# A ring of 27 banks of exponentials in place of a scaled copy of V, with a second side bank and no credit rule in the last sets

## The chip, the cores and the metric

The kernel runs on one core of one Trainium2 chip. The metric is the device time of one execution in microseconds (us). Runs of a kernel are summed up by their median.

## The reference

One transformer block with adaptive layer norm: S = 2048 tokens, D = 512, H = 32 heads of 16, F = 1792, all in bf16.

```python
mod = (silu(c) @ w_mod) -> sa, ca, ga, sb, cb, gb        # six rows of 512
h = layernorm(x) * (1 + ca) + sa
q, k, v = split(h @ wqkv)                                 # 32 heads, Dh = 16
p = softmax(q @ k.T * Dh ** -0.5)                         # 2048 x 2048 for each head
x = x + ga * (concat(p @ v) @ wo)
h = layernorm(x) * (1 + cb) + sb
x = x + gb * ((gelu(h @ w_gate) * (h @ w_up)) @ w_down)
```

## The kernel before

**Tiles and sets.** The 2048 queries are cut into seven sets: two of 512 tokens, three of 256, two of 128 (`SETS`). A unit is one set and one group of four heads (`qd`, eight of them); the two last sets share their first five units, which are 256 wide. A unit walks over the keys in rounds. A round is four banks, one per head, of 128x512 scores. In all there are 2048 banks, in a fixed order; `pos` is the number of banks issued so far, and `ends[k]` the position at which set k is done. `ends[4]` is 1792: the last two sets are the last 256 banks.

**From scores to PV.** TensorE writes scores (QK) to `scp`, six PSUM banks used as two groups of three in turn. ScalarE takes a group's banks in one exponential and writes them to `E`, a ring of `NSL` = 12 banks in SBUF. TensorE then multiplies them with V (`vaug`, which has a column of ones for the denominator) and accumulates in `pv`, one PSUM bank. QK of a group is issued only when the ring has free places for it, that is, when the rounds that held these places have been through PV.

**Vector rounds.** Some rounds are made on VectorE instead. Of a group of three banks ScalarE then takes two, and VectorE the third. One TENSOR_SCALAR turns scores into the bits of a bf16 number y whose exponent is right and whose mantissa is linear (`BITS_C`). When four banks are there (128x2048), three more steps follow (`power_task`): `mant` keeps y's mantissa bits and sets the exponent of one (a mask and an OR), `square` multiplies that with y, and `expo` keeps only y's exponent (a mask). The power of two is the sum of both, the square times 0.496 and the exponent part times one. So such a round goes through PV twice: the exponent part with `vaug`, the square with `vs`, a copy of V scaled by `SQUARE_W`. The copies are made by `scale_v`, 16 instructions, each after its part of V. A vector round is opened only when VectorE's queue is short, buffers are free, no earlier one is overdue, V's scaled copy is there, and, from `LATE_AT` = `ends[4]` on, when the credit of the side work is under `CREDIT` = 1024. Only a full group of three can give a bank to VectorE.

**Side work.** Everything else (projections of later heads, output projection, layer norm, FFN of finished sets) is a list of generators. Each yields matmuls into one PSUM bank, `mi`, and then empties it with VectorE instructions. Side work earns credit with every bank of scores, by what is left of it and when it is due, and spends it in TensorE columns; a high credit means that it is behind. TensorE is kept awake with filler matmuls on the identity when its recent work falls under a bound (`FILL`).

**Order.** The program is one list per engine, put in order by a scheduler in the kernel file, which keeps modelled times of all engines (`free`, `probe`). At each step it issues QK as soon as its banks and places are free, else PV, side work or filler. The scheduler runs when the kernel is built; the chip runs the finished lists, with semaphores.

**End.** The last sets' leftovers are run by `tail`: output projection and FFN of the last set, mixed with the rest of the FFN of the set before it.

All matmuls are recorded by line 318, all ScalarE instructions by line 336, and on VectorE two-tensor operations by line 340, tensor-scalar ones by 348, copies by 357. So groups of one line are told apart by tile names.

Of the kernel before, what the change touches and what calls it, by code (L numbers as in the profile page):

```python
# [6 lines left out]
ALU = mybir.AluOpType  # L7
# [9 lines left out]
H = 32  # L17
# [17 lines left out]
QS = 5  # L35
CH = 3
SC = 2 * CH
NSL = 12
assert NSL % CH == 0
LEAD = 5  # L40
CREDIT = 1024
LATE_AT = lambda ends: ends[4]
AHEAD = 24
NEAR = 8
FIRST = 0
# [12 lines left out]
EXP_SCALE = float(np.log(2.0) / OCT)  # L58
Q_SCALE = float(0.25 * np.log2(np.e) * OCT)

SQUARE_W = 0.49609375
BITS_C = float(128 * (127 - 0.58035))
MANT, ONE, EXPO = 0x7F, 0x3F80, 0xFF80

COMPUTE = ("pe", "act", "dve", "pool")
ALLENG = ("sp",) + COMPUTE
# [362 lines left out]
class _Kernel(_Recorder):  # L429
# [12 lines left out]
    def alloc(self):  # L442
# [32 lines left out]
        self.bufs += [(mreg[:, 4096 + 2048 * i:6144 + 2048 * i], "modB") for i in range(4)]  # L475
        self.bufs.append((wreg[:, 4096:6144], ("q", 3, 3)))
        self.held = set()
        self.flowing = self.closing = False
        self.vs = sb("vs", [P, NKT, H * VW], BF16)
        self.wo = sb("wo", [P, 8, D], BF16)  # L480
        self.E = sb("E", [P, NSL, 512], BF16)
        self.onorm = sb("onorm", [P, 8, 512], BF16)
# [232 lines left out]
    def side_v(self, g, dc):  # L715
        mi = self.mi[:, :]

        def part(t):
            for dci in range(NDC):
                self.mm(mi[:, P * t:P * t + P], self.hT[:, dci, 512 * g + P * t:512 * g + P * t + P],  # L720
                        self.wqkv[:, dci, 1024 + P * dc:1024 + P * dc + P],
                        start=(dci == 0), stop=(dci == NDC - 1))
        for t in range(4):
            yield 512, lambda t=t: part(t)
        dst = self.vaug[:, 4 * g:4 * g + 4, VW * 8 * dc:VW * 8 * dc + VW * 8]
        self.copy("dve", dst.rearrange("p t (h c) -> p t h c", c=VW)[:, :, :, 0:DH],
                  mi.rearrange("p (t h c) -> p t h c", t=4, c=DH))
        self.done(("v", g, dc))
        if not self.dry:
            self.task([lambda: self.scale_v(g, dc)], ("vs", g, dc))  # L730
        yield END

    def scale_v(self, g, dc):
        t, c = slice(4 * g, 4 * g + 4), slice(VW * 8 * dc, VW * 8 * dc + VW * 8)
        self.ts("dve", self.vs[:, t, c], self.vaug[:, t, c], SQUARE_W, None, ALU.mult)

    def side_t(self, src, n, h, out, mod):
        pt = self.mi[:, :].bitcast(BF16)
        w = P * n

        def part(i):
            for t in range(n):
                self.transpose(pt[:, w * i + P * t:w * i + P * t + P],
                               src(t)[:, P * (2 * h + i):P * (2 * h + i) + P], self.ident[:, :])
        for i in range(2):
            yield w, lambda i=i: part(i)
        for i in range(2):
            dc = 2 * h + i
            self.modulate("dve", out(dc), pt[:, w * i:w * i + w], mod, dc)
        yield END  # L750

    def after(self, keys):
        return lambda: all(k in self.have for k in keys)
# [135 lines left out]
    def side_wo(self, gi):  # L889
        q0, W = SETS[gi]  # L890
        n = W // P
        tiles = [q0 // P + i for i in range(n)]
        mi = self.mi[:, :]
        yield from self.until("wo")
        for i in range(n):
            for qd in range(8):
                yield from self.until(("onorm", gi, qd))
                yield 512, lambda i=i, qd=qd: self.wo_mm(mi, gi, i, qd)
            self.wo_fin(mi, tiles[i])
            if not self.dry:  # L900
                self.task([lambda t=tiles[i]: self.ln_stat(t)], ("st2", tiles[i]))
            yield END
        if not self.dry:
            self.done(("wo", gi))
            self.task(self.ln2_steps(gi), ("ln2", gi), self.after([("st2", t) for t in tiles]))

    def side_ffn(self, gi, part=None):
# [1 line left out]
        q0, W = SETS[gi]  # L909
        n = W // P  # L910
        tiles = [q0 // P + i for i in range(n)]
        mi = self.mi[:, :]
        c0 = BCOL[gi]
        prod = self.prodT if W == 512 else self.prodL
        flow = gi < FLOW
# [32 lines left out]
            yield from self.side_t(lambda t: self.normed(gi, t), n, h,  # L948
                                   lambda dc: self.t2T[:, dc, c0:c0 + W], self.modB)

        def up(x, ci, sub, after=()):
            for s, fc in enumerate(sub):
                for dci in range(NDC):
                    if flow:
                        lhs = ring[(nch * x + ci) % 4][:, dci, P * (fc % 2):P * (fc % 2) + P]
                    else:
                        lhs = self.up_w((self.wg, self.wu)[x], fc, dci)
                    yield W, lambda s=s, lhs=lhs, dci=dci, aft=after if s == dci == 0 else (): self.mm(
                        mi[:, W * s:W * s + W], lhs, self.t2T[:, dci, c0:c0 + W], start=(dci == 0), stop=(dci == NDC - 1),
                        after=aft)  # L960
# [11 lines left out]
        if part is not None:  # L972
            for ci in range(part):
                fcs = chunks[ci]
                m = len(fcs)
                g, w = self.gw[:, ci % 2, 0, 0:m * W], self.gw[:, ci % 2, 1, 0:m * W]
                yield from up(0, ci, fcs)
                self.copy("dve", g, mi[:, 0:W * m])
                if not self.dry:
                    self.task([lambda g=g, w=w: self.tt("dve", w, g, g, ALU.mult),  # L980
                               lambda w=w: self.ts("dve", w, w, GELU_C, 1.0, ALU.mult, ALU.add),
                               lambda g=g, w=w: self.tt("dve", w, w, g, ALU.mult),
                               ("act", lambda w=w: self.act(w, w, ACT.Tanh, scale=TANH_C0))], ("gelu", gi, ci))
                yield END
            for ci in range(part):
                fcs = chunks[ci]
                m = len(fcs)
                g, w = self.gw[:, ci % 2, 0, 0:m * W], self.gw[:, ci % 2, 1, 0:m * W]
                yield from self.until(("gelu", gi, ci))
                yield from up(1, ci, fcs)  # L990
                self.stt(w, w, 1.0, mi[:, 0:W * m], ALU.add, ALU.mult)
                self.stt(place(fcs), split(w, m), 0.5, split(g, m), ALU.mult, ALU.mult)
                yield END
            self.done(("part", gi))
            return
        for i in range(3):
            load_down(i)
        for ci in range(len(chunks)):
            for sub in banks(ci):
                yield from up(0, ci, sub)  # L1000
                self.copy("dve", place(sub), split(mi[:, 0:W * len(sub)], len(sub)))
                yield END
            load(ci + 4)
# [3 lines left out]
        yield from self.until(("gelu", gi))  # L1007
        for ci in range(len(chunks)):
            for sub in banks(ci):
                yield from up(1, ci, sub, (place(sub),))  # L1010
                self.tt("dve", place(sub), split(mi[:, 0:W * len(sub)], len(sub)), place(sub), ALU.mult)
                yield END
            load(nch + ci + 4)
        for i in range(n):
            for fc in range(NFC):
                yield 512, lambda i=i, fc=fc: self.mm(
                    mi, prod[:, fc, P * i:P * i + P], (self.wdst if flow else self.wd)[fc // 2][:, fc % 2, :], start=(fc == 0), stop=(fc == NFC - 1))
            self.down_fin(mi, tiles[i])
            yield END
# [124 lines left out]
    def stream(self):  # L1144
        self.split = True
        self.tasks = []
        self.task([lambda: self.scale_v(0, 0)], ("vs", 0, 0))
        self.live = {}
        self.have = {("k", 0, 0), ("q", 0, 0), ("v", 0, 0)}
        self.credit = 0  # L1150
# [132 lines left out]
        while cg <= group[units[-1]]:  # L1283
# [8 lines left out]
            self.background(t)  # L1292

            tq = None
            mem, after = take(CH - 1 if pos < nsplit + 12 and c % 2 else CH)
            s0 = CH * (c % 2)
            if mem:
                e0 = 0 if e + len(mem) > NSL else e
                if all(owner.get(e0 + i, -1) < rp for i in range(len(mem))):
                    tq = self.probe(lambda: self.mm(self.scp[:, s0:s0 + CH, 0:P], *filler))  # L1300
            if tq is not None and tq <= t + 30:
                slack = self.free["act"] - 600 - t
                w = self.next_side()
# [7 lines left out]
                if len(mem) == CH and ("k", 3, 0) in self.have and self.free["dve"] < max(t + 400, self.free["act"]) + 500:  # L1311
# [4 lines left out]
                        if not overdue - {quad["rnd"][0]}:  # L1316
                            g = pick(quad)
                    elif (not overdue and cand and len(self.spare()) > 1 and (pos < LATE_AT(ends) or self.credit < CREDIT) and rounds[cand[0]][2] < pos + 96 and self.backlog() < BACK
                          and ("vs", rounds[cand[0]][1] * (512 // rounds[cand[0]][0][3]) // 4, rounds[cand[0]][0][1] // 2) in self.have
                          and all(k in self.have for k in self.keys(seq[rounds[cand[0]][2]]))):  # L1320
                        rnd = rounds[cand.pop(0)]
                        quad = {"rnd": rnd, "j": [0, 1, 2, 3], "k": self.spare()[0], "ready": [], "n": 2, "slot": None}
# [83 lines left out]
    def pv_mms(self, rnd, acc, src, i, first, last):  # L1406
# [2 lines left out]
        dc, ee = qd // 2, qd % 2  # L1409
        for kk in range(kpb):  # L1410
            kt = r * kpb + kk
            v = (self.vs if i else self.vaug)[:, kt, :]
            for j in range(4):
                h = 8 * dc + 2 * j + ee
                self.mm(acc[32 * j:32 * j + VW, 0:W], v[:, VW * h:VW * h + VW], src[j][:, W * kk:W * kk + W],
# [7 lines left out]
    def power_task(self, q):  # L1423
# [5 lines left out]
            return self.bufs[self.spare()[0] if q["slot"] is None else q["slot"]][0]  # L1429

        def mant():
            self.ts("dve", slot().bitcast(U16), y.bitcast(U16), MANT, ONE, ALU.bitwise_and, ALU.bitwise_or)
            if self.probing is None:
                q["slot"] = self.spare()[0]
                self.held.add(q["slot"])
# [4 lines left out]
                q["ready"].append((1, quarters(slot())))  # L1440

        def expo():
            self.ts("dve", y.bitcast(U16), y.bitcast(U16), EXPO, None, ALU.bitwise_and)
            if self.probing is None:
                q["ready"].append((0, quarters(y)))
        self.task([mant, square, expo], ("shift", q["rnd"][0]),
# [55 lines left out]
    def tail(self, ka, kb):  # L1502

        self.require([("part", ka)])
        self.split = False
        self.act(self.tcol[:, 0:1], self.tcol[:, 0:1], ACT.Gelu_apprx_tanh)
        gens = [self.tail_end(kb), self.tail_ffn(ka, self.pv[:, :], range(0, 4), 0)]
# [140 lines left out]
```

## Time and profile before

| what | us |
|---|---|
| median of 3 runs (lowest, highest) | 856.21 (853.2, 856.58) |
| the profiled execution's own time | 852.99 |
| its span, first to last instruction | 851.2 |
| ScalarE busy | 810.5 (95%) |
| TensorE busy | 747.1 (88%) |
| VectorE busy | 724.0 (85%) |
| mean granted TensorE clock | 0.997 |

The time of an execution is its span and 1.8 us around it. Busy shares are means over the whole span; the stages differ, which the views by stretches of time show. Groups of instructions give the count, the busy time, the mean of one, and the idle time of their engine just ahead of them with what ended it.

### The profile page before, as it was taken

The numbers are of one execution on the slowest core, as the hardware profiler recorded it, in microseconds if no ns is written. First come the engines' busy times: TensorE is split into PE (matmuls) and PEld (weight loads), VectorE is DVE, ScalarE is ACT, GpSimd is POOL, SyncE is SP. The second block draws the span as 40 slices with busy tenths as digits, with TensorE's granted clock in tenths as the row PEclk, the third lists the DMA queues.
The fourth block names the chain that finished last, engine by engine and source line by source line (L and its number), as shares of the span: only waits on it lengthen the run. The fifth ranks groups of instructions, "written<-read, shape, count | busy, mean of one in ns | idle before, by whom it ended". The sixth has DMA issues, their size and how long they took to land.

```text
span 851.2 us, 29704 instructions
## 1 busy us (share of the span) xinstructions
PE 747.1 (88%) x13466; PEld 292.1 (34%) x13471; DVE 724.0 (85%) x1307; ACT 810.5 (95%) x738; POOL 4.5 (1%) x12
## 2 busy tenths in 40 slices
PE   7888989888888978899998989998898889888887
PEld 3333232322222222222333323433443443344455
DVE  7857999999999987999999999999898989735764
ACT  5999999999999999999999999999998999999982
POOL 1000000000000000000000000000000000000000
PEclk9999999999999999999999999999999999999999
DMA  8100000000012111110003212103451431500000
GB/s 284 39 25 13 9 9 9 10 9 8 9 45 66 55 35 33 46 33 21 23 9 94 71 45 55 48 23 105 122 155 47 144 97 55 144 10 6 22 6 13
DMA packets 76360, 43.71 MB, mean 51 GB/s; under 512 B 20557, under 2 KB 74634, under 8 KB 76234
## 3 DMA queue, kind: packets, MB, share of 16 engines
q1 hardware_dynamic: 76232, 41.82, 17.4%
q8 instruction: 105, 1.72, 0.8%
q14 instruction: 21, 0.17, 0.1%
q10 hardware_dynamic: 2, 0.00, 0.0%
HBM read 39.18 MB, written 2.61 MB: 49 GB/s over the span
## 4 chain that ended last, share of the span: by engine, by line
ACT 69%; PE 14%; DVE 9%; DMA 4%; SPq 1%; issue 1%; DVEq 0%
ACT E L336 66%; PE ps_mi L318 6%; PE ps_sc L318 6%; PE ps_pv L318 2%; ACT hreg L336 2%; DVE mreg L348 2%; DMA rb<-scr_rec 1%; DMA scr_rec<-rden 1%; ACT L336 1%; SPq L386 1%; DMA den<-scr_den 1%; DMA scr_den<-osb 1%; DVE mreg L340 1%; DVE dreg L348 1%; DVE hreg L357 1%
## 5 line engine op out<-in xcount | busy, mean ns | idle before, releaser
L336 ACT ACTIVATE E<-ps_sc 128x1024 bf16<-128x1024 f32 (+2 forms) x698 | 765.1, 1294 | 19.2 <-PE ps_sc L318 18.5
L318 PE MATMUL ps_sc<-qT,kmo 32*128 32x256 bf16 (+2 forms) x1664 | 194.3, 299 | 21.9 <-ACT E L336 19.5
L318 PE MATMUL ps_sc<-qT,kme 32*128 32x256 bf16 (+2 forms) x1600 | 188.4, 304 | 26.8 <-ACT E L336 23.8
L348 DVE TENSOR_SCALAR mreg<-ps_sc 128x512 uint16<-128x512 f32 x232 | 157.1, 686 | 23.6 <-PE ps_sc L318 21.4
L318 PE MATMUL ps_pv<-E,vaug 128*17 128x256 bf16 (+2 forms) x2620 | 165.9, 300 | 8.3 <-DVE osb L357 4.3
L318 PE MATMUL ps_mi<-wreg,mreg 128*32 128x256 bf16 (+2 forms) x2048 | 112.0, 319 | 17.6 <-DVE hreg L340 8.5
L348 DVE TENSOR_SCALAR dreg<-ps_sc 128x512 uint16<-128x512 f32 x140 | 94.8, 686 | 14.7 <-PE ps_sc L318 13.0
L318 PEld LDWEIGHTS ps_sc<-qT,kme 32*128 32x128 bf16 x1600 | 51.8, 92 | 140.0 <-ACT E L336 116.2
L318 PEld LDWEIGHTS ps_sc<-qT,kmo 32*128 32x128 bf16 x1664 | 54.5, 92 | 123.8 <-ACT E L336 90.6
L318 PEld LDWEIGHTS ps_pv<-E,vaug 128*17 128x17 bf16 x2620 | 55.1, 89 | 86.6 <-issue 47.2
L318 PEld LDWEIGHTS ps_mi<-wreg,mreg 128*32 128x32 bf16 x2048 | 44.1, 95 | 57.4 <-issue 17.5
L348 DVE TENSOR_SCALAR mreg<-mreg 128x2048 uint16<-128x2048 uint16 x86 | 58.3, 681 | 0.1
L340 DVE TENSOR_TENSOR hreg<-ps_mi,hreg 128x512 bf16<-128x512 f32 x49 | 33.6, 685 | 13.8 <-PE ps_mi L318 13.7
L357 DVE CAST hreg<-ps_mi 128x512 bf16<-128x512 f32 x49 | 33.6, 685 | 10.3 <-PE ps_mi L318 10.1
L318 PE MATMUL ps_mi<-hreg,wreg 128*32 128x512 bf16 x480 | 38.4, 383 | 1.2 <-DVE vaug L357 0.5
L318 PE MATMUL ps_mi<-wo,onorm 128*32 128x512 bf16 x480 | 37.0, 383 | 1.8 <-DVE xs L340 1.4
L340 DVE TENSOR_TENSOR dreg<-mreg,dreg 128x2048 bf16<-128x2048 bf16 x30 | 36.4, 1215 | 0.0
L318 PE MATMUL ps_mi<-xs,ident 128*32 128x512 bf16 x412 | 32.6, 382 | 1.9 <-DVE hreg L357 1.1
L340 DVE TENSOR_TENSOR mreg<-mreg 128x2048 bf16<-128x2048 bf16 x28 | 33.9, 1212 | 0.1
L340 DVE TENSOR_TENSOR mreg<-dreg,mreg 128x2048 bf16<-128x2048 bf16 x27 | 32.8, 1215 | 0.1
L318 PE MATMUL ps_mi<-mreg,hreg 128*32 128x512 bf16 x384 | 32.4, 384 | 0.0
L340 DVE TENSOR_TENSOR onorm<-osb,rb 128x256 bf16<-128x256 f32 (+2 forms) x51 | 24.6, 485 | 8.7 <-DMA rb<-scr_rec 8.5
(159 smaller groups left out, 684.7 us busy)
## 6 DMA issues: line engine op xcount, KB each, us to landing
mreg<-in_B_w_up_dram SPq DMA_DIRECT2D x32, 256.0 KB, 3.0
mreg<-in_B_w_gate_dram SPq DMA_DIRECT2D x28, 256.0 KB, 3.3
mreg<-in_B_w_down_dram SPq DMA_DIRECT2D x16, 256.0 KB, 2.8
dreg<-in_B_w_down_dram SPq DMA_DIRECT2D x12, 256.0 KB, 5.3
mreg<-in_w_mod_dram SPq DMA_DIRECT2D x1, 2048.0 KB, 12.0
rb<-scr_rec SPq DMA_DIRECT2D x64, 32.0 KB, 1.8
out_dram<-xs SPq DMA_DIRECT2D x16, 128.0 KB, 1.8
rb<-scr_rec SPq DMA_DIRECT2D x116, 16.0 KB, 1.7
```

Of the source, the lines that this page charges most:

```text
L318: return self.rec("pe", lambda e: e.matmul(out, lhsT, rhs, start=start, stop=stop, tile_position=tp), [lhsT, rhs, *after], [out], cost=(n, ...
L336: return self.rec("act", lambda e: e.activation(out, in_, func, scale=scale, **kw), rd, wr, cost=self.cost("act", out, [in_], "act") + load)
L340: return self.rec(eng, lambda e: e.tensor_tensor(out, a, b, op), [a, b], [out], cost=self.cost(eng, out, [a, b], "tt"))
L348: return self.rec(eng, lambda e: e.tensor_scalar(out, a, s1, s2, **kw), rd, [out], cost=self.cost(eng, out, [a], "ts") + (60 if len(rd) > ...
L357: return self.rec(eng, lambda e: e.tensor_copy(out, in_), [in_], [out], cost=self.cost(eng, out, [in_], "ts"))
L386: return e.dma_start(out, in_)
```

## The change

- `vs` and `scale_v` go. The factor is put into the masks: `mant` now sets the exponent of one half (`HALF`), so that the square is halved, and `expo` sets the lowest mantissa bit (`UNIT`), which multiplies the exponent part by 1 + 1/128. The ratio of both is as before, and the common factor is taken out in `BITS_C`. Both PV passes use `vaug`, and a vector round waits for its part of `vaug` instead of `vs`.
- The memory of `vs` (17,408 bytes of each partition) becomes ring: `NSL` is 27, 15 banks of 1024 bytes more.
- `CREDIT` is 5000. The credit is held to 4096 at most, so the rule is never in force.
- From `TWO_AT` = `ends[4]` until the tail, side work uses `mi` and the last bank of `scp` in turn (`bank()`), and every second group has two banks instead of three, as in the first stage, where that bank is the accumulator of a second unit.

```diff
-NSL = 12
+NSL = 27
-CREDIT = 1024
+CREDIT = 5000
 LATE_AT = lambda ends: ends[4]
+TWO_AT = lambda ends: ends[4]
...
-SQUARE_W = 0.49609375
-BITS_C = float(128 * (127 - 0.58035))
-MANT, ONE, EXPO = 0x7F, 0x3F80, 0xFF80
+BITS_C = float(128 * (127 - 0.58035 - np.log2(1 + 2.0 ** -7)))
+MANT, HALF, EXPO, UNIT = 0x7F, 0x3F00, 0xFF80, 0x0001
...
-        self.vs = sb("vs", [P, NKT, H * VW], BF16)
+        self.two = self.flip = False
...
-        if not self.dry:
-            self.task([lambda: self.scale_v(g, dc)], ("vs", g, dc))
...
-    def scale_v(self, g, dc):
-        t, c = slice(4 * g, 4 * g + 4), slice(VW * 8 * dc, VW * 8 * dc + VW * 8)
-        self.ts("dve", self.vs[:, t, c], self.vaug[:, t, c], SQUARE_W, None, ALU.mult)
...
+    def bank(self):
+        if self.dry or not self.two:
+            return self.mi[:, :]
+        self.flip = not self.flip
+        return self.scp[:, SC - 1, :] if self.flip else self.mi[:, :]
...
-        mi = self.mi[:, :]
         yield from self.until("wo")
         for i in range(n):
+            mi = self.bank()
...
-                yield from up(0, ci, fcs)
+                mi = self.bank()
+                yield from up(mi, 0, ci, fcs)
...
-            mem, after = take(CH - 1 if pos < nsplit + 12 and c % 2 else CH)
+            self.two = pos >= TWO_AT(ends)
+            mem, after = take(CH - 1 if (pos < nsplit + 12 or self.two) and c % 2 else CH)
...
-                    tq = self.probe(lambda: self.mm(self.scp[:, s0:s0 + CH, 0:P], *filler))
+                    tq = self.probe(lambda: self.mm(self.scp[:, s0:s0 + len(mem), 0:P], *filler))
...
-                          and ("vs", rounds[cand[0]][1] * (512 // rounds[cand[0]][0][3]) // 4, rounds[cand[0]][0][1] // 2) in self.have
+                          and ("v", rounds[cand[0]][1] * (512 // rounds[cand[0]][0][3]) // 4, rounds[cand[0]][0][1] // 2) in self.have
...
-            v = (self.vs if i else self.vaug)[:, kt, :]
+            v = self.vaug[:, kt, :]
...
-            self.ts("dve", slot().bitcast(U16), y.bitcast(U16), MANT, ONE, ALU.bitwise_and, ALU.bitwise_or)
+            self.ts("dve", slot().bitcast(U16), y.bitcast(U16), MANT, HALF, ALU.bitwise_and, ALU.bitwise_or)
...
-            self.ts("dve", y.bitcast(U16), y.bitcast(U16), EXPO, None, ALU.bitwise_and)
+            self.ts("dve", y.bitcast(U16), y.bitcast(U16), EXPO, UNIT, ALU.bitwise_and, ALU.bitwise_or)
...
 def tail(self, ka, kb):
         self.require([("part", ka)])
+        self.two = False
```

More of the change, by code (lines that the diff above doesn't have):

```diff
@@ L728, in side_v @@
         self.done(("v", g, dc))
-        if not self.dry:
-            self.task([lambda: self.scale_v(g, dc)], ("vs", g, dc))
         yield END
-    def scale_v(self, g, dc):
-        t, c = slice(4 * g, 4 * g + 4), slice(VW * 8 * dc, VW * 8 * dc + VW * 8)
-        self.ts("dve", self.vs[:, t, c], self.vaug[:, t, c], SQUARE_W, None, ALU.mult)
     def side_t(self, src, n, h, out, mod):
-        pt = self.mi[:, :].bitcast(BF16)
+        pt = self.bank().bitcast(BF16)
         w = P * n
@@ L911, in side_ffn @@
         tiles = [q0 // P + i for i in range(n)]
-        mi = self.mi[:, :]
         c0 = BCOL[gi]
@@ L949, in side_ffn, with up @@
                                    lambda dc: self.t2T[:, dc, c0:c0 + W], self.modB)
-        def up(x, ci, sub, after=()):
+        def up(mi, x, ci, sub, after=()):
             for s, fc in enumerate(sub):
@@ L989, in side_ffn @@
                 yield from self.until(("gelu", gi, ci))
-                yield from up(1, ci, fcs)
+                mi = self.bank()
+                yield from up(mi, 1, ci, fcs)
                 self.stt(w, w, 1.0, mi[:, 0:W * m], ALU.add, ALU.mult)
@@ L999, in side_ffn @@
             for sub in banks(ci):
-                yield from up(0, ci, sub)
+                mi = self.bank()
+                yield from up(mi, 0, ci, sub)
                 self.copy("dve", place(sub), split(mi[:, 0:W * len(sub)], len(sub)))
@@ L1009, in side_ffn @@
             for sub in banks(ci):
-                yield from up(1, ci, sub, (place(sub),))
+                mi = self.bank()
+                yield from up(mi, 1, ci, sub, (place(sub),))
                 self.tt("dve", place(sub), split(mi[:, 0:W * len(sub)], len(sub)), place(sub), ALU.mult)
@@ L1014, in side_ffn @@
         for i in range(n):
+            mi = self.bank()
             for fc in range(NFC):
@@ L1146, in stream @@
         self.tasks = []
-        self.task([lambda: self.scale_v(0, 0)], ("vs", 0, 0))
         self.live = {}
```

## The prediction

> **What bounds the kernel now.** I read the page first, for the engine that is never free.
>
> ```profile
> span 851.2 us, 29704 instructions
> PE 747.1 (88%) x13466; PEld 292.1 (34%) x13471; DVE 724.0 (85%) x1307; ACT 810.5 (95%) x738; POOL 4.5 (1%) x12
> L336 ACT ACTIVATE E<-ps_sc 128x1024 bf16<-128x1024 f32 (+2 forms) x698 | 765.1, 1294 | 19.2 <-PE ps_sc L318 18.5
> ```
>
> ScalarE is busy for 810.5 of 851.2 us, and 765.1 of that are exponentials. Little else is left in its row. A change gains by making ScalarE do fewer banks, by filling its few holes, or by shortening what stands behind its last exponential.
>
> Second, the groups by shape, which price one bank (128x512 scores) on either engine:
>
> ```profile
> L336 ACT ACTIVATE E<-ps_sc 128x1536 bf16<-128x1536 f32 x292 | 416.8, 1551 | 4.0 <-PE ps_sc L318 3.8
> L336 ACT ACTIVATE E<-ps_sc 128x1024 bf16<-128x1024 f32 x400 | 392.4, 1119 | 7.9 <-PE ps_sc L318 7.6
> L348 DVE TENSOR_SCALAR mreg<-ps_sc 128x512 uint16<-128x512 f32 x232 | 157.1, 686 | 23.6 <-PE ps_sc L318 21.4
> L348 DVE TENSOR_SCALAR mreg<-mreg 128x2048 uint16<-128x2048 uint16 x86 | 58.3, 681 | 0.1
> L340 DVE TENSOR_TENSOR dreg<-mreg,dreg 128x2048 bf16<-128x2048 bf16 x30 | 36.4, 1215 | 0.0
> L348 DVE TENSOR_SCALAR vs<-vaug 128x544 bf16<-128x544 bf16 x16 | 4.4, 282 | 0.1
> ```
>
> Three banks against two differ by 1551 - 1119 = 432 ns, which is the price of a bank on ScalarE. The instructions overlap, so the fixed part comes from the sum: 292 x 3 + 400 x 2 = 1676 banks x 0.432 = 724 us of the 765.1, and 41 us over 698 instructions is 0.059 us each. A vector round (four banks) costs VectorE 4 x 0.686 + 2 x 0.681 + 1.215 = 5.32 us and relieves ScalarE of 4 x 0.432 = 1.73 us.
>
> Third, busy time in stretches of 20 us, for the place where VectorE is not full (columns PE, PEld, DVE, ACT), and the same for the score banks alone, where the DVE count is the vector banks:
>
> ```profile
> 700.00:720.00 20.00, 18.96 (x405) 8.13 (x400) 18.05 (x29) 18.52 (x18) 0.00 (x0) 1.00 0.23 66
> 740.00:760.00 20.00, 18.06 (x432) 9.12 (x428) 10.30 (x29) 20.00 (x16) 0.00 (x0) 1.00 0.05 10
> 760.00:780.00 20.00, 15.79 (x396) 8.49 (x390) 10.93 (x18) 19.95 (x17) 0.00 (x0) 1.00 0.03 7
> 780.00:800.00 20.00, 18.61 (x520) 9.53 (x520) 12.08 (x23) 19.79 (x19) 0.00 (x0) 1.00 0.08 21
> 800.00:820.00 20.00, 17.53 (x580) 10.05 (x580) 11.88 (x33) 20.00 (x16) 0.00 (x0) 1.00 0.05 9
> ...
> 700.00:720.00 20.00, 6.92 (x108) 2.08 (x108) 7.77 (x12) 18.52 (x18) 1.00 0.23 66
> 740.00:760.00 20.00, 7.17 (x112) 2.08 (x112) 0.00 (x0) 20.00 (x16) 1.00 0.05 10
> 760.00:780.00 20.00, 5.13 (x88) 1.84 (x82) 2.74 (x4) 14.11 (x13) 1.00 0.03 7
> 780.00:800.00 20.00, 6.79 (x188) 3.63 (x188) 5.42 (x8) 19.79 (x19) 1.00 0.08 21
> 800.00:820.00 20.00, 8.42 (x212) 3.92 (x208) 0.00 (x0) 20.00 (x16) 1.00 0.05 9
> ```
>
> Before 720 both engines are nearly full. From 740 to 820 ScalarE stays full, but VectorE idles 9.7 + 9.1 + 7.9 + 8.1 = 34.8 us and takes only 12 banks. This is the stage of the last sets, where the credit rule forbids new vector rounds. The order of VectorE shows the hole itself:
>
> ```profile
> 732.29 0.69 DVE L348 TENSOR_SCALAR dreg<-dreg 128x2048 uint16<-128x2048 uint16 x1
> 759.74 0.69 DVE L357 CAST hreg<-ps_mi 128x512 bf16<-128x512 f32 x1 [1.50 <-PE ps_mi L318]
> 761.59 0.69 DVE L357 CAST hreg<-ps_mi 128x512 bf16<-128x512 f32 x1 [1.17 <-PE ps_mi L318]
> 770.77 1.49 DVE L348 TENSOR_SCALAR mreg<-ps_sc 128x512 uint16<-128x512 f32 x2 [1.71 <-PE ps_sc L318]
> ```
>
> From 732.29 + 0.69 to 770.77, 38 us, no vector bank is made. The two casts show the side work on its single bank: a bank is emptied every 1.85 us, 1.17 us of which VectorE waits for TensorE, and TensorE may refill only after the 0.69 us cast.
>
> **The ring and V's second copy.** ScalarE's holes are short; between 40 and 160, then between 160 and 720:
>
> ```profile
> ACT E L336 <- PE ps_sc L318: 1.2, 2, 0.8
> ...
> ACT E L336 <- PE ps_sc L318: 8.3, 11, 1.5
> ```
>
> The longest kind, at the end of a unit, in order of time:
>
> ```profile
> 713.87 0.39 PE L318 MATMUL ps_sc<-qT,kme 32*128 32x256 bf16 x6
> ...
> 715.50 0.39 PE L318 MATMUL ps_pv<-dreg,vaug 128*17 128x256 bf16 x8
> ...
> 716.36 0.42 DVE L357 COPY osb<-ps_pv 128x256 f32<-128x256 f32 x1
> 716.84 0.40 PE L318 MATMUL ps_pv<-E,vaug 128*17 128x256 bf16 x8 [0.30 <-DVE osb L357]
> 717.16 0.28 PE L318 MATMUL ps_sc<-qT,kme 32*128 32x256 bf16 x2
> 717.60 1.94 ACT L336 ACTIVATE E<-ps_sc 128x1024 bf16<-128x1024 f32 x2 [1.48 <-PE ps_sc L318]
> ```
>
> Scores are made at 713.87 and then not until 717.16. In between the old unit's last vector round must be multiplied with V, its accumulator copied out at 716.36, and the new unit's first round read at 716.84; only then are ring places free, because QK is issued only for free places. Twelve banks cover four groups; 27 cover nine or more, so this hole should go. What is late next is TensorE, which at 18.96 of 20 us there has little to spare. Of 1.2 + 8.3 = 9.5 us I take two thirds as gone, 6.3 us; the bounds are 9.5 and, if TensorE rather than the ring is late, nothing or a loss of 2 us from a longer backlog of PV at the ends of units.
>
> Dropping the scaled V removes 16 x 0.282 us, the row's 4.4 us of VectorE. In a stage where VectorE is full, this is 4.4 / 5.32 = 0.83 vector rounds, or 0.83 x 1.73 = 1.4 us of ScalarE; the other bound is nothing, if the freed time is not picked up. The new masks cost nothing: the step that clears the exponent already has AND and OR in one instruction, the other has AND alone, and the group of 86 that holds both has one mean, 681 ns. PV with the plain V instead of the scaled one reads the same shape. V needs only its own copy now, not the scaling behind it, before a vector round may open.
>
> **The last sets.** What follows the last exponentials keeps its length:
>
> ```profile
> 795.13 0.69 DVE L340 TENSOR_TENSOR wreg<-ps_mi,gb 128x512 bf16<-128x512 f32 x1
> 806.56 0.29 DVE L357 COPY osb<-ps_pv 128x128 f32<-128x128 f32 x1 [1.28 <-PE ps_pv L318]
> 822.99 1.51 ACT L336 ACTIVATE E<-ps_sc 128x1536 bf16<-128x1536 f32 x1
> 826.11 0.28 DVE L357 COPY osb<-ps_pv 128x128 f32<-128x128 f32 x1
> 828.32 0.69 DVE L353 SCALAR_TENSOR_TENSOR hreg<-wreg 128x512 bf16<-128x512 bf16 x1
> ```
>
> The set before the last finishes attention at 806.56, and its normalization, projection and first FFN chunks run until 829.0. That is 22 us of dependent steps, later than the last exponential at 824.5. Faster exponentials in the last 48 banks would only make the chain end last; gains ahead of 806 shift it whole. The 25 us tail from 826.11 to the span's end at 851.2 I leave alone.
>
> Where do the last 256 banks begin? From 740 to 824.5 there are 84.5 us, less the 19.95 - 14.11 = 5.84 us that the stretch from 760 has of other ScalarE work: 78.7 us, at 0.432 + 0.059 / 2.8 = 0.453 us a bank 174 banks, with the 12 vector banks 186. The other 70, eight of them vector banks as I estimate, take 62 x 0.453 = 28 us: they begin at about 712. So five vector rounds lie behind position 1792 now, and the 38 us hole will be open to more. While the second side bank is in use, odd groups have two banks, both for ScalarE, and only even groups can give one to VectorE, so at most one bank in five: 51 of 256, twelve rounds. VectorE's idle time from 740 to 820 would hold 34.8 / 5.32 = 6.5 rounds more. The casts and normalizations come at their own times, and the scheduler opens a round only with VectorE's queue short, so I take 5 more. One of these should fall in the last 48 banks, where it gains nothing (above). Four count: 4 x 1.73 = 6.9 us. The ends are no more rounds, and 6.5 x 1.73 = 11.2 us.
>
> Against that, smaller groups mean more instructions. With ten vector rounds the 216 banks left go in 40 pairs of groups of 2 and 2, and 56 banks as 3 and 2, 80 + 22 = 102 instructions; before, 20 groups of two beside a vector bank and 196 / 3 = 65 of three, 85. So 17 more x 0.059 = 1.0 us. The Trainium skill, Perfetto Trace Analysis, section Optimizing Scalar/DVE Operations, says that larger operations help where the engine is saturated, which speaks against these groups; its page ScalarE: Activation LUTs, section What ACT_TABLE_LOAD costs, gives an ACTIVATE without pointer operands 186 ns beside its elements, with 93 ns of overlap, so 93 ns where the rows give 59. By the page the estimate is 17 x 0.093 = 1.6 us, 0.6 us more in the sum; the rows decide.
>
> Each vector round adds one more pass of PV on TensorE, a pair of stretches like the 0.39 us one at 715.50 in place of one. Five passes are 2 us in 80, and fillers are there to give way:
>
> ```profile
> 740.00:760.00 20.00, 2.41 (x28) 0.80 (x28) 0.00 (x0) 1.00 0.05 10
> ...
> 800.00:820.00 20.00, 4.43 (x52) 1.10 (x48) 0.00 (x0) 1.00 0.05 9
> ```
>
> These rows are the matmuls on the identity, nearly all fillers. The second side bank lets TensorE fill one bank while VectorE empties the other. The side work is not what ends last now, so I count it at nothing, but it pays for the casts that will stand behind vector work. If that cover fails, the rival below follows.
>
> **Sum.** -6.3 (ring), -1.4 (scaled V), -6.9 (four rounds), +1.0 (smaller groups) = -13.6 us. The profiled execution took 852.99 us, so 839.4. The median of the runs, 856.21, stands 3.2 above it, so I forecast 842.6; the rivals' times are given by the median too.
>
> **Rivals.** The first needs the count of side results, VectorE's instructions on the side bank in the first and the last of five stretches (the five have 35):
>
> ```profile
> 740.00:760.00 20.00, 8.71 (x208) 4.84 (x204) 5.87 (x11) 0.00 (x0) 1.00 0.05 10
> ...
> 820.00:840.00 20.00, 4.07 (x194) 3.10 (x190) 2.96 (x4) 0.00 (x0) 1.00 0.04 11
> ```
>
> First, the side work becomes the bound (slower). The last FFN that must precede the 806.56 chain ends at 795.13 + 0.69, so about 10.7 us of slack. Each of the 35 may stand behind a vector step of 0.68 to 1.22 us. If each loses 0.8 us that the second bank doesn't hide, that is 28 us, less 10.7 us of slack and less the ring's 6.3 and V's 1.4: +9.6 us, 866. It decides from 18.4 / 35 = 0.53 us each. For it: VectorE takes its queue in order, and the two casts above follow one another by dependence. Against it: with two banks 0.7 us or more of each 1.85 us cycle is hidden, and the 10.7 us slack.
>
> Second, no change. The holes are TensorE's, not the ring's, and in the last sets only one of the four rounds counts, as two-bank groups leave TensorE 0.432 us less to come back with scores: -1.4 - 1.73 + 1.0 = -2.1 us, 854. For it: PE at 18.96 of 20 where the hole of 717.60 lies. Against: the scores stop there for 3.3 us while PV of the old unit goes on, which is what a full ring looks like.
>
> Third, the ring alone works: VectorE's scheduler finds no room in the last sets, as its other conditions (backlog, waiting rounds, the 24 banks ahead) take the credit's place. -6.3 - 1.4 + 1.0 = -6.7 us, 849.5. Against it: one row of four banks at 770.77 starts as soon as credit falls, so the rule was what barred it.
>
> Fourth, more: the longer ring also lets rounds be opened earlier all through, and all bounds come in: -9.5 - 1.4 - 11.2 + 1.0 = -21.1 us, 835. For it: VectorE waits 21.4 us for scores in the row of 232 vector banks. Against it: before 720 it is nearly full already.
>
> **How the numbers follow.** Forecast 0.50, first rival 0.14, second 0.13, third 0.15, fourth 0.08. About 0.5% or 4.3 us is what a measurement can tell from no change, so below 851.9 counts as faster: 0.50 + 0.08 + 0.15 = 0.73. Same 0.13, slower 0.14. The range leaves out most of the first rival and the far end of the fourth: from 832, the bounds below 835 with the spread of the runs (3.4 us), to 857, past the second rival.
>
> **What would show it.** Right: ScalarE's idle time behind scores falls from 9.5 to about 3 us between 40 and 720; no row writes the scaled V; from 740 to 820 VectorE's count of score banks rises from 12 to some 30, and the last exponential ends 12 to 14 us earlier; the distance from it to the end stays near 27 us. Wrong: the holes at unit ends stay with 27 banks; ScalarE shows idle time behind scores from 740 on, with two-bank groups; or the projection and FFN of the set before the last end further than 5 us behind the last exponential.

## The result and the profile after

| what | before | after |
|---|---|---|
| median, us (first comparison) | 855.64 | 846.91 |
| ratio of the two, 95% interval | | 0.9891 [0.9854, 0.9928] |
| profiled execution, us | 852.99 | 842.79 |
| its span, us | 851.2 | 841.1 |

The time fell by 8.7 us where 13.6 were forecast, and 846.91 lies in the range of 832 to 857. A second comparison, with more runs (e1 below), gives 6.0 us, so the change is worth some 6 to 9 us. The page after, its span, busy times and group of exponentials:

```profile
span 841.1 us, 29493 instructions
PE 740.7 (88%) x13350; PEld 289.5 (34%) x13355; DVE 732.6 (87%) x1312; ACT 805.8 (96%) x755; POOL 4.5 (1%) x12
L336 ACT ACTIVATE E<-ps_sc 128x1024 bf16<-128x1024 f32 (+2 forms) x715 | 760.1, 1281 | 12.0 <-PE ps_sc L318 11.7
```

The exponentials lost 5.0 us of busy time and 7.2 us of idle time ahead of them. Together that is 12.2 us, of which the span shows 10.1: about 2 us came back behind the last exponential. ScalarE's waits for scores after the change, between 40 and 160, then between 160 and 720:

```profile
ACT E L336 <- PE ps_sc L318: 0.4, 1, 0.4
...
ACT E L336 <- PE ps_sc L318: 2.5, 4, 0.8
```

9.5 us became 2.9 us in this execution. The vector banks from 740 to 820, where there were 12 (two rows, by the tile written), and the stretches of the last sets (PE, PEld, DVE, ACT):

```profile
L348 DVE TENSOR_SCALAR mreg<-ps_sc 128x512 uint16<-128x512 f32 x12 | 8.3, 688 | 3.3 <-PE ps_sc L318 3.0
L348 DVE TENSOR_SCALAR dreg<-ps_sc 128x512 uint16<-128x512 f32 x5 | 3.4, 687 | 1.0 <-PE ps_sc L318 1.0
...
740.00:760.00 20.00, 19.07 (x490) 11.05 (x486) 17.29 (x33) 19.97 (x20) 0.00 (x0) 1.00 0.05 11
760.00:780.00 20.00, 18.48 (x450) 9.53 (x438) 12.13 (x19) 19.99 (x21) 0.00 (x0) 1.00 0.06 13
780.00:800.00 20.00, 17.17 (x552) 10.09 (x543) 13.45 (x25) 18.93 (x20) 0.00 (x0) 1.00 0.09 17
800.00:820.00 20.00, 16.64 (x552) 10.73 (x554) 13.29 (x37) 14.62 (x16) 0.00 (x0) 1.00 0.03 6
```

17 banks, not some 30. VectorE is still a third idle from 760 on. The end, as ScalarE and VectorE have it:

```profile
797.67 14.20 ACT L336 ACTIVATE E<-ps_sc 128x1536 bf16<-128x1536 f32 x13 [1.07 <-PE ps_sc L318]
...
791.76 0.29 DVE L357 COPY osb<-ps_pv 128x128 f32<-128x128 f32 x1 [0.24 <-PE ps_pv L318]
...
800.17 0.28 DVE L340 TENSOR_TENSOR onorm<-osb,rb 128x128 bf16<-128x128 f32 x1
802.52 0.69 DVE L340 TENSOR_TENSOR xs<-xs,ps_mi 128x512 bf16<-128x512 bf16 x1 [2.06 <-PE ps_mi L318]
...
817.70 0.69 DVE L353 SCALAR_TENSOR_TENSOR hreg<-wreg 128x512 bf16<-128x512 bf16 x1
```

The last exponential ends at 811.9, 12.6 us earlier than before; the span's end follows 29.2 us later instead of 26.7. The chain of the set before the last takes 26.6 us from the last copy of its accumulator (791.76) to its last FFN product (818.4), where it took 22.4. That product now ends 6.5 us behind the last exponential; before, it was 4.5 us.

The kernels of this table are put on one scale by ScalarE's position: the time at which its groups of exponentials, counted up to that time, reach the number of banks that the program's order gives it up to bank 1792 (the last two sets begin) and bank 2000 (the last 48). Rounds are vector rounds in that order; "to" and "behind" mean bank 1792. Times in us, of each profiled execution.

| kernel | rounds to 1792, behind | to 1792 | 1792 to 2000 | to the last exponential | behind it | span |
|---|---|---|---|---|---|---|
| before | 86, 7 | 712.0 | 91.7 | 20.8 | 26.7 | 851.2 |
| after | 87, 9 | 703.9 | 85.8 | 22.2 | 29.2 | 841.1 |
| e1 whole again | 87, 9 | 705.5 | 87.8 | 21.9 | 30.2 | 845.4 |
| e2 masks | 86, 6 | 712.5 | 88.9 | 25.3 | 23.3 | 850.0 |
| e3 + ring | 87, 4 | 702.5 | 94.3 | 25.8 | 23.0 | 845.6 |
| e4 + side bank, no rule | 86, 10 | 712.8 | 89.0 | 18.9 | 31.2 | 851.9 |
| f1 + ring, no rule | 87, 13 | 703.2 | 80.2 | 18.9 | 49.0 | 851.3 |
| f2 + ring, side bank | 87, 5 | 703.8 | 91.3 | 26.1 | 22.8 | 844.0 |

Up to bank 1792 every kernel of the table with 27 banks runs the same order, so 702.5 to 705.5 is also the scatter of one program. It moves with the granted clock, as the last section tells. From before to after, the stretches of the table give -8.1 us to bank 1792, -5.9 to bank 2000, +1.4 to the last exponential and +2.5 behind it.

### The profile page after: what moved, and what is told of

It is laid out like the page before. It is cut to its first block, busy times and chain, and to the rows that moved or that the text cites. A ratio compares the mean times of both kernels' runs of the same rounds, so it can differ in the third digit from the quotient of the medians.

```text
span 841.1 us, 29493 instructions
## 1 busy us (share of the span) xinstructions
PE 740.7 (88%) x13350; PEld 289.5 (34%) x13355; DVE 732.6 (87%) x1312; ACT 805.8 (96%) x755; POOL 4.5 (1%) x12
## 4 chain that ended last, share of the span: by engine, by line
ACT 84%; PE 8%; DMA 3%; DVE 3%; issue 1%; SPq 1%; DVEq 0%
ACT E L336 81%; PE ps_sc L318 4%; PE ps_mi L318 3%; ACT hreg L336 2%; DMA scr_rec<-rden 1%; DMA rb<-scr_rec 1%; ACT L336 1%; PE ps_pv L318 1%; SPq L386 1%; DVE dreg L348 0%; DVE hreg L357 0%; DVE mreg L348 0%; DVE wreg L340 0%; DVE dreg L340 0%; DVE onorm L340 0%
## 5 line engine op out<-in xcount | busy, mean ns | idle before, releaser
L336 ACT ACTIVATE E<-ps_sc 128x1024 bf16<-128x1024 f32 (+2 forms) x715 | 760.1, 1281 | 12.0 <-PE ps_sc L318 11.7
L318 PE MATMUL ps_sc<-qT,kmo 32*128 32x256 bf16 (+2 forms) x1664 | 203.0, 299 | 26.2 <-ACT E L336 24.0
L318 PE MATMUL ps_sc<-qT,kme 32*128 32x256 bf16 (+2 forms) x1600 | 200.8, 306 | 28.4 <-ACT E L336 25.5
L348 DVE TENSOR_SCALAR mreg<-ps_sc 128x512 uint16<-128x512 f32 x244 | 164.9, 687 | 24.6 <-PE ps_sc L318 21.3
L318 PE MATMUL ps_pv<-E,vaug 128*17 128x256 bf16 (+2 forms) x2596 | 152.3, 300 | 3.1 <-DVE osb L357 2.2
L318 PE MATMUL ps_mi<-wreg,mreg 128*32 128x256 bf16 (+2 forms) x1920 | 109.0, 326 | 10.4 <-DVE hreg L340 5.0
L318 PEld LDWEIGHTS ps_sc<-qT,kme 32*128 32x128 bf16 x1600 | 55.0, 92 | 143.6 <-ACT E L336 122.6
L348 DVE TENSOR_SCALAR mreg<-mreg 128x2048 uint16<-128x2048 uint16 x91 | 61.7, 682 | 0.3
L318 PE MATMUL ps_pv<-mreg,vaug 128*17 128x256 bf16 (+2 forms) x728 | 44.9, 304 | 4.1 <-DVE mreg L340 2.4
L318 PE MATMUL ps_sc<-xs,ident 128*32 128x512 bf16 x276 | 22.4, 385 | 10.6 <-ACT E L336 10.3
```

The source lines that it names most:

```text
L318: return self.rec("pe", lambda e: e.matmul(out, lhsT, rhs, start=start, stop=stop, tile_position=tp), [lhsT, rhs, *after], [out], cost=(n, ...
L336: return self.rec("act", lambda e: e.activation(out, in_, func, scale=scale, **kw), rd, wr, cost=self.cost("act", out, [in_], "act") + load)
L348: return self.rec(eng, lambda e: e.tensor_scalar(out, a, s1, s2, **kw), rd, [out], cost=self.cost(eng, out, [a], "ts") + (60 if len(rd) > ...
```

## The experiments

**The parts, run together: e1, e2, e3, e4.** e1 is the whole change again. The others take parts of it back. Each group of experiments ran beside its own runs of the kernel before, so across groups the ratios are compared and not the medians:

```diff
 # e2_masks
-NSL = 27
+NSL = 12
-CREDIT = 5000
+CREDIT = 1024
-TWO_AT = lambda ends: ends[4]
+TWO_AT = lambda ends: 1 << 30
 # e3_ring: the last two of these edits; e4_two_credit: the first alone
```

> The whole change again, beside its parts. All theories: about 9 us under the kernel before (ratio 0.989). The count of vector rounds is 96 against 93.

> Only the masks: no scaled V, ring of 12, credit rule and single side bank as before. Theory (each part as the prediction had it): VectorE loses 4.4 us of work, worth at most 1.4 us; 0 to -1.4 us against before. Rival (the scaled V held back vector rounds early on): -3 us or more, with at least two rounds more.

> Masks and ring of 27, the last sets as before. Theory: ScalarE's idle time behind scores between 40 and 720 us falls from 9.5 us to about 3, and the time falls by 6 to 8 us against before, most of the whole change. Rival (the holes are TensorE's, and the gain comes from the last sets): -2 us or less, idle time above 6 us.

> Masks, second side bank and no credit rule, with the ring of 12. Theory: only the last sets gain, -2 to -4 us against before, and ScalarE's idle time between 40 and 720 us stays near 9 us. Rival (the last sets carry the gain): -7 us or more.

| kernel | median us | ratio to before | interval |
|---|---|---|---|
| e1 whole | 847.06 | 0.9925 | [0.9902, 0.9949] |
| e2 masks | 851.85 | 0.9988 | [0.9970, 1.0006] |
| e3 masks, ring | 850.47 | 0.9964 | [0.9938, 0.9989] |
| e4 masks, side bank, no rule | 852.34 | 0.9997 | [0.9980, 1.0013] |

e1: 6.0 us by the medians, where the first comparison gave 8.7; the intervals of the two overlap.

e2: the masks alone can't be told from no change by the ratio. The order has 92 vector rounds, one fewer than before, so the 4.4 us freed on VectorE were not picked up as a round. But its runs had a lower granted clock than those of the kernel before (median 0.992 against 0.997). At one clock it is some 4 us faster, as the next section tells, and what makes that is not shown.

e3: ScalarE's waits for scores between 40 and 712 are 2.5 us; with the ring of 12 in e4 they are 8.5:

```profile
ACT E L336 <- PE ps_sc L318: 2.5, 5, 0.8
...
ACT E L336 <- PE ps_sc L318: 8.5, 16, 1.3
```

The same unit's end in both shows the hole itself. In e4 its accumulator is copied out at 651.05, and ScalarE waits for the new unit's scores:

```profile
651.05 0.41 DVE L357 COPY osb<-ps_pv 128x256 f32<-128x256 f32 x1
...
652.36 4.20 ACT L336 ACTIVATE E<-ps_sc 128x1536 bf16<-128x1536 f32 x4 [1.16 <-PE ps_sc L318]
```

In e3 the copy stands at 643.95, and ScalarE runs through it:

```profile
633.00 18.18 ACT L336 ACTIVATE E<-ps_sc 128x1536 bf16<-128x1536 f32 x15
...
643.95 0.42 DVE L357 COPY osb<-ps_pv 128x256 f32<-128x256 f32 x1 [0.22 <-PE ps_pv L318]
```

So the holes were the ring's, and in e3's profile bank 1792 comes 10 us earlier than in e2's (712.5 to 702.5). Not all of it is the ring's: up to there e2 ran 13.7 us at half the clock, and e3 3.4 us. But the time fell by 0.36%, 3 us, and not the 6 to 8 expected. Two things took it back. Under the credit rule the order has 4 vector rounds behind 1792 instead of 6, and the stretch to bank 2000 takes 94.3 us instead of 88.9. The other is a lower granted clock in most runs (median 0.988; last section).

e4: the last exponential comes 6.0 us earlier than in e2 (820.7 against 826.7), and the tail behind it is 7.9 us longer. Nothing is left. ScalarE's end there:

```profile
793.67 27.01 ACT L336 ACTIVATE E<-ps_sc 128x1024 bf16<-128x1024 f32 x27 [1.01 <-PE ps_sc L318]
820.64 0.63 ACT L336 ACTIVATE wreg<-wreg 128x512 bf16<-128x512 bf16 x1
824.76 0.63 ACT L336 ACTIVATE wreg<-wreg 128x512 bf16<-128x512 bf16 x1 [3.49 <-DVE wreg L340]
```

When the exponentials are done, ScalarE waits 3.49 us for the FFN of the set before the last. Against e2, ring and last sets alone give -1.4 and +0.5 us by the medians; both give -4.8. They are worth more together than apart.

**Side bank and rule, one without the other: f1, f2.**

```diff
 # f1_ring_credit: the whole change, but
-TWO_AT = lambda ends: ends[4]
+TWO_AT = lambda ends: 1 << 30
 # f2_ring_two: the whole change, but
-CREDIT = 5000
+CREDIT = 1024
```

> Masks, ring of 27, no credit rule, but one side bank to the end. The order then has 13 vector rounds in the last 256 banks, against 9 in the whole change and 7 before. Theory (the side work on one bank becomes what ends last when VectorE takes more): slower than the whole change by 4 to 10 us, although ScalarE has 6.9 us less to do; the last exponential comes earlier, and the FFN of the set before the last ends more than 8 us behind it. Rival (ScalarE decides, the second bank is in the way of vector rounds): faster than the whole change by 4 us or more.

> Masks, ring of 27 and second side bank, with the credit rule. The order has 5 vector rounds in the last 256 banks, against 9 in the whole change. Theory (rounds decide what the last sets give): 4 x 1.73 = 6.9 us more for ScalarE than in the whole change, of which 2 to 5 us show, the rest being hidden by the chain of the set before the last. Rival (the second bank alone makes the gain of the last sets, as it frees the side work): within 1.5 us of the whole change.

f1: 857.35 us, 1.0030 [1.0000, 1.0059]; f2: 851.52 us, 0.9965 [0.9946, 0.9984]. f1 has 13 vector rounds behind 1792, and its last exponential ends at 802.3, the earliest of all. Then ScalarE stands still:

```profile
794.02 8.29 ACT L336 ACTIVATE E<-ps_sc 128x1536 bf16<-128x1536 f32 x6
823.52 0.63 ACT L336 ACTIVATE wreg<-wreg 128x512 bf16<-128x512 bf16 x1 [21.20 <-DVE wreg L340]
```

For 21.2 us it waits for side work; the tail is 49.0 us. This is the prediction's first rival, where the second bank is missing. Not all of the 49 us is that wait's: from 800 to 820 TensorE was busy for 11.2 us, and its mean granted clock was 0.78 there and 0.88 from 820 to 840. f1 also has four rounds more than the whole change, 13 against 9, so the missing bank and the added rounds are not told apart. f2 has the second bank and keeps the rule: the same ratio as e3, so on top of the ring the bank alone gains nothing. Only the pair pays. f2 against the whole change tells how much the four rounds more (9 against 5) give without the rule: 0.9965 against 0.9925 and 0.9891, 3 to 6 us of 6.9.

**The size of the ring: f3, g4.** `NSL = 18` in the whole change and in the next kernel, f4.

> The whole change with a ring of 18. Theory: the hole at a unit's end lasts 3.3 us, some seven banks of ScalarE's work, so a ring of 18 covers it: within 2 us of the whole change. Rival (the gain grows with every bank of the ring): a gain of some 6.5 x 6/15 = 2.6 us over the ring of 12, so 4 us slower than the whole change.

> As g2_near5_again with a ring of 18. Theory (18 places cover the holes at unit ends): within 2 us of g2. Rival (the gain grows with every bank): 3 to 4 us slower.

f3: 0.9888 [0.9850, 0.9926]; g4: 846.28 us, 0.9894 [0.9859, 0.9930], beside 845.92 for the ring of 27. The last nine banks move nothing in the time that these runs can tell; the order with 18 also has one vector round more, 97. In the traces they do move something. The waits for scores between 40 and 712 are 4.7 us in f3, and with 27 they are 2.5 to 5.9 us, depending on the profiled execution. But the kinds differ. Of the waits over 0.2 us between 40 and 790, those that end within 3.5 us of a copy of an accumulator come to 6.8 us before the change, 5.4 in e2 and 6.0 in e4 (12 places), 4.5 in f3 and 3.6 in g4 (18), and none in the whole change, e1 and e3 (27; g1, whose order has more fillers, has 2.5). So 18 places leave over half of the holes at the ends of units. Much of what remains with 27 stands in or next to stretches of half clock (last section): 3.9 of 5.6 us in e1, 4.4 of 5.7 in g2.

**The chain at the end: f4, g2, g3.** In f4 and g2 the unit whose result came at 800.17 by DMA is normalized through TensorE:

```diff
-        if sets[0] >= len(SETS) - 2 and len(sets) == 1 and qd >= 6:
+        if sets[0] >= len(SETS) - 2 and len(sets) == 1 and qd >= (5 if sets[0] == len(SETS) - 2 else 6):
...
+        w.append((lambda: self.near_end(k, 5, self.mi[:, 0:P]), s0, s0))
         w.append((lambda: self.near_end(k, 6, self.mi[:, 0:P]), s0, s0))
 # g3_near5_late in addition
-LATE_AT = lambda ends: ends[4]
+LATE_AT = lambda ends: ends[5] - 48
-CREDIT = 5000
+CREDIT = -1e9
```

> The whole change, but the sixth unit of the set before the last is normalized through TensorE (as its seventh and eighth units are) and not through four steps of DMA. Theory (the chain of that set now ends last, and its latest input is the one that came by DMA at 800.17 us): 2 to 4 us faster than the whole change. Rival (the last exponential still decides): no change within 1 us.

> The whole change with the sixth unit of the set before the last normalized through TensorE, again, beside the three others. 2 to 3 us under the whole change's 847, ratio to the kernel before about 0.987 (its first runs gave 0.986).

> As g2_near5_again, but no vector round is opened in the last 96 banks (from position 1952 on): 7 and 0 rounds in the last two stretches instead of 8 and 1. Theory (the last exponentials have slack against the dependent chain, and vector rounds there stand in the chain's way on VectorE): within 1 us of g2, the tail behind the last exponential 2 to 4 us shorter, the last exponential 2 to 4 us later. Rival (ScalarE decides to the end): 2 x 1.73 = 3.5 us slower than g2.

f4: 844.39 us, 0.9863 [0.9836, 0.9890]; g2: 845.92 us, 0.9882 [0.9845, 0.9920]. Both lie below the whole change's two ratios. f4's interval stays clear of e1's, but overlaps that of the first comparison, and g2's median is only 1 us from e1's; so 2 to 4 us are not shown. In g2's trace the chain itself is shorter: the sum of projection and input (`xs`) comes at 801.29, where e1 has it at 805.83, and the last FFN product ends at 817.2 instead of 821.0. Yet the spans are 845.2 and 845.4 us. From 816 on, g2 ran at a mean clock of 0.88 and e1 at 0.92, which may hide part of what the chain gained. g3: 847.06 us, 0.9894 [0.9859, 0.9929]. The last exponentials of g2, then of g3:

```profile
814.46 1.52 ACT L336 ACTIVATE E<-ps_sc 128x1024 bf16<-128x1024 f32 x2
...
816.91 4.00 ACT L336 ACTIVATE E<-ps_sc 128x1024 bf16<-128x1024 f32 x4
```

They end at 816.0 and 820.9, and both spans are 845.2 us: 4.9 us of ScalarE's end left no trace in the span, and the medians are 1.1 us apart. This fits slack in the last exponentials. It is not proof, since the mean clock from 816 to 845 was 0.88 in g2 and 0.94 in g3.

**Fillers: g1.** `FILL = 4800` in the whole change, in place of 4200.

> The whole change with the bound under which fillers are issued raised from 4200 to 4800 columns in 3.4 us (it changes the order a little: 96 vector rounds, as in the whole change). The runs of kernels with the ring of 27 showed granted clocks of 0.985 to 0.992, those of the kernel before 0.992 to 1.000, and within one kernel the time rises as the clock falls, some 0.55 us for 0.001. Theory (part of the gain is lost in a lower clock, as TensorE has more short idle stretches): the clock is 0.993 or more and the median 2 to 4 us under the whole change's 847. Rival (the clock is not set by fillers here, and fillers stand in QK's way): clock as before it, time equal or up to 3 us longer.

845.98 us, 0.9878 [0.9841, 0.9914]. The median granted clock of its runs is 0.994, against 0.988 and 0.990 for the whole change's two series. Against the whole change the time fell by 1 us by the medians, and by 1 to 4 us by the ratios. The clock followed the fillers, but the order changed too, and the intervals overlap; the 2 to 4 us are neither shown nor excluded. No version clearly beats the whole change.

## Why the prediction was right, and where it was not

- **Ring, -6.3: right as to the wait.** ScalarE's waits between 40 and 720 fell by 6.6 us, and the hole at the ends of units is gone with 27 banks and present with 12 (e2, e4). The second rival, that TensorE makes the holes, falls. In time the ring alone gave less, 1.4 us more than the masks (e3 against e2).
- **Scaled V, -1.4: not shown.** e2's interval holds both this and nothing; no more rounds appear in its order. At one clock e2 gains 4.4 us, more than the term, by a way that the prediction doesn't have.
- **Four counting rounds of five, -6.9: mis-sized.** The order gained two rounds behind 1792 (7 to 9), not five; two are 3.5 us. (The prediction's five rounds before the change are those made after 712, by which time two of the seven were done.) The stretch from 1792 to 2000 fell by 5.9 us, which also holds the 2.3 us less of the waits from 712 to 790 that the prediction did not price. The step that failed is the one that filled VectorE's idle time with rounds. With one bank in five for VectorE, rounds come slowly, and here even slower than that (vector banks alone):

```profile
725.01 0.69 DVE L348 TENSOR_SCALAR dreg<-ps_sc 128x512 uint16<-128x512 f32 x1 [0.77 <-PE ps_sc L318]
...
729.11 0.69 DVE L348 TENSOR_SCALAR dreg<-ps_sc 128x512 uint16<-128x512 f32 x1 [1.32 <-PE ps_sc L318]
...
730.94 0.69 DVE L348 TENSOR_SCALAR dreg<-ps_sc 128x512 uint16<-128x512 f32 x1 [0.21 <-PE ps_sc L318]
...
735.21 0.69 DVE L348 TENSOR_SCALAR dreg<-ps_sc 128x512 uint16<-128x512 f32 x1
```

  A bank came mostly every 2 or 4 us, so a round of four took 10 to 17 us in this stage, where it took 3 to 5 us before the change, and only one is open at a time. The same rules without the second bank gave 13 rounds (f1). Why chances were missed was not tried.
- **Smaller groups, +1.0: right in count.** 715 instructions against 698 are the 17 forecast. 2048 - 4 x 96 = 1664 banks x 0.432 + 715 x 0.059 = 761.0 us; measured 760.1. The estimate of 93 ns from the Trainium skill, ScalarE: Activation LUTs, section What ACT_TABLE_LOAD costs, would make 785 us; the trace decides for 59 ns in this stream.
- **The tail keeps its length: wrong by 2.5 us.** The chain of the set before the last grew from 22.4 to 26.6 us; its latest input was the unit normalized by DMA (800.17). Its FFN ended 6.5 us behind the last exponential, and more than 5 us was one of the prediction's own signs of being wrong. Where exponentials come sooner the tail is longer: 23 us with the credit rule, 29 to 31 with the pair, 49 with rounds and one bank. Part of the gain of the rounds is paid back there.
- **First rival (side work becomes the bound): it does not decide the whole change, but it shows in f1,** at 857 us where it said 866. The cover that the prediction named, the second bank, stands between the two, and so do four rounds.
- **Third rival (no room for rounds): half of it came.** Two rounds of five appeared. 846.9 us lies nearer to this rival's 849.5 than to the forecast 842.6, and e1's 6.0 us are under half of the forecast. Its other half, that the ring alone makes the gain, does not hold (e3).
- **Profile and median.** The forecast carried the 3.2 us between them over. The gap was 4.1 us, part of which is the clock.

The profiled executions differ by 10.2 us where 13.6 were forecast. The rounds that did not come (3.4 us) and the longer tail (2.5 us), less the unpriced waits (2.3 us), are 3.6 us. That this meets the 3.4 us that are missing so closely is chance, since the clock alone moves an execution by more. So the ring's mechanism was right; the time came inside the range with one term at half its size, a tail that grew, and one term that is not shown.

What stays open: why ring and last sets give 4.8 us together and 0.9 apart. At a clock of 0.992, by a line through each kernel's runs, the kernel before stands at 856.0 us, and e2, e3, e4 and e1 at 851.6, 847.9, 851.5 and 844.9. The masks are then worth 4.4 us, the ring 3.7 us on top of them, and the pair 0.1 without the ring and 3.0 with it. The first of these was not expected: at 0.992 itself, six runs of the kernel before took 854.4 to 857.8 us, and five of e2 850.1 to 852.0. Such a comparison takes the clock as given from outside; where a kernel's order itself makes the clock fall, the fall belongs to the kernel. The order differs in every kernel, so no single wait could be named.

## What to carry to other kernels

A deeper ring pays where the profile shows the producer stopped while an old unit drains; half as many places again (18 for 12) gave the same time here, although the trace still shows holes. Work moved off the busiest engine near the end is worth only what the dependent chain behind it doesn't need: look first at how far that chain ends behind the busy engine. A rule that holds work back and a buffer that makes room for it are tried together: beside the ring alone, the bank gave nothing, and taking the rule away gave a loss.

## What was not expected of the hardware

The granted clock moves these times from run to run. Over 35 runs of the kernel before, the time rises by 0.63 us for each 0.001 that the clock falls (850.3 us at 1.000, 861.7 at 0.986), and over 12 runs of the whole change by 0.52. The changed kernels ran at lower clocks than the 0.997 of before beside them: medians of 0.988 with 27 places (e1, e3), 0.992 and 0.990 with 12 (e2, e4). By these lines the change lost some of its gain there; g1 raised the clock but did not show the gain.

In all profiled executions the clock has two levels. It stands at 1.00 and falls to 0.50 for 3.4 or 6.8 us at a time (a fall at the span's end can be shorter), so e1's mean of 0.987 is six such falls. Some come back at the same place of an order: eight of the nine profiled kernels with 27 places fall near 320 us, and none of the five with 12 or 18.

The clock also falls without a long idle stretch. After the change, the ten us ahead of this fall and those of the fall, and TensorE's longest idle time ahead of it:

```profile
310.00:320.00 10.00, 6.27 (x90) 1.64 (x89) 7.16 (x11) 9.98 (x6) 0.00 (x0) 1.00 0.03 4
320.00:330.00 10.00, 8.97 (x81) 2.00 (x78) 7.97 (x14) 8.64 (x10) 0.00 (x0) 0.66 0.16 41
...
319.07 0.39 PE L318 MATMUL ps_sc<-qT,kme 32*128 32x512 bf16 x3 [1.62 <-ACT E L336]
```

TensorE was busy for 6.27 of ten us, with no gap above 1.62 us, and then ran at a mean clock of 0.66; ScalarE lost 1.4 us in that stretch. The Trainium skill, TensorE: Matmul & The Clock Gate, section What's actually happening, puts the fall behind an idle window of some 3.4 us. Here no such gap stands in the trace, so a kernel can't count gaps alone. Thinness alone does not tell either: the kernel before was busy for 3.71 of the seven us from 316 to 323, less than the 4.25 of 313 to 320 here, and its clock stayed at 1.00. What sets the fall stays open.
